# Moving the block means of v from the sync queue to GpSimd's DMA queue in a fused attention, expert and feed-forward kernel

## The chip, the cores and the metric

One core of a Trainium2 chip runs the whole program. The metric is device time in microseconds (us) of one execution; three executions of the kernel before are given, and one execution was also taken by the hardware profiler. The engines are TensorE (PE in the profile), VectorE (DVE), ScalarE (ACT), GpSimd (POOL) and SyncE (SP). SP and POOL also issue DMAs: those of SP are the queue "q1 hardware_dynamic" of the profile, those of POOL "q0 software_dynamic".

## The reference, cut to what matters

Attention over 2 batches of 8 heads, 768 positions of 64 numbers. Each position looks at the 31 positions of a band around it and at 24 summaries, one for each block of 32 positions. A block's summary key is the maximum of its keys, its summary value the mean of its values:

```python
k_sum = k.reshape(B, H, nb, block, D).max(axis=3)
v_sum = v.reshape(B, H, nb, block, D).mean(axis=3)
...
scores_all = np.concatenate([scores_l_m, scores_s], axis=-1)
...
v_all = np.concatenate([v, v_sum], axis=2)
return np.matmul(a, v_all)
```

The 1536 resulting tokens of 512 numbers go through a mixture of 8 experts (one per token, 512 to 1024 to 512) and then through a second feed-forward layer (512 to 2048 to 512). The change touches the attention alone, and in it the way of `v_sum` into the matrix product.

## The kernel before

**Attention.** Two heads lie side by side on the 128 partitions: that makes 8 pairs of heads, n = 0 to 7. A pair's 768 queries are 12 tiles of 64, worked on in groups of 4 tiles: three groups a pair, g = 0, 1, 2. Group i = 3n + g; the last group of the last pair is cut in two, so there are 25. The order of all work is written out by hand in the loop `for i in range(G)` (line 569). Iteration i transposes the exponentials of group i-2 (`do_t`), makes the scores of group i (`do_s`, line 360), the output product of group i-3 (`do_o`, line 401), the transposes of the output of group i-4 (`do_x`, line 429) and the gate product of group i-5. Each engine takes its instructions strictly in the order in which this loop names them, and waits at one until its inputs are there.

**What the output product reads.** `vw` holds, for one pair, on 24 partitions the block means, repeated for each of the 12 tiles, and on 96 partitions the windows of v, which a load (`load_v`, line 294) brings. There are three `vw` buffers, used in turn. The means come about in four steps. `vsum(n)` adds up the 32 values of a block: on DVE for n = 0 and 1, from n = 2 on in five halving steps on POOL (line 307), from `vk`, a second layout of v that `load_vk` (line 291) brings, with the block and the quarter of the columns on 96 partitions. `vmean(n)` scales by 1/32 on DVE (line 312) and issues on SP a DMA that brings the 96 x 32 means to 24 partitions of 128 numbers (`vt<-vs`, line 314): 96 runs of 128 bytes, in all 12 KB. `put_vsum(n)` issues on SP a DMA that writes each of the 24 rows twelve times into `vw` (`vw<-vt`, line 317): 288 runs of 512 bytes, 144 KB. The second DMA needs what the first one wrote, so SP waits for it to land before it issues the second.

**What else SP issues.** At the start of a pair (g = 0), right behind `put_vsum(n)`: keys and queries of pair n+2 (`wf<-in_kt` 128 x 800, `wf<-in_qt` 128 x 768, lines 260 and 261), `vk` of pair n+2 (96 x 1024) and the windows of pair n+1 (96 x 1548). At g = 2 it stores the finished output of pair n-1 to memory in two DMAs of 192 KB (line 420). Each SP DMA also waits until the one issued eight earlier has landed. `put_vsum(n)` stands at iteration 3n and is needed by `do_o` of iteration 3n+3; `vmean(n+1)` stands at g = 2 of pair n, `vsum(n+1)` at g = 1. POOL also copies the keys of each group into place (`kt<-wf`, line 282), two iterations ahead of their use. At iteration 18 SP begins to load the first expert's weights (`load_ahead`, lines 129 and 134), whose rounding copies run on DVE (line 563) from iteration 21 on, and the first gather of tokens (line 161) is an indirect DMA on POOL's queue.

**After the attention** come the routing of the tokens, 13 slots of 128 tokens through the experts, and the second layer; the functions of the change are not called there.

Of the kernel before, what the change touches and what calls it, by code (L numbers as in the profile page):

```python
# [26 lines left out]
P = 128  # L27
# [14 lines left out]
# columns of the float32 constants  # L42
# [44 lines left out]
def tile_kernel(ctx: ExitStack, tc: tile.TileContext, a, out, dbg=None):  # L87
# [3 lines left out]
    # ---- pools that live through the kernel  # L91
# [19 lines left out]
    # ---- moe2 weights: float64 bits to float32  # L111
# [46 lines left out]
    # ---- a slot of 128 tokens of one expert  # L158
# [61 lines left out]
    # ================= attention =================  # L220
# [5 lines left out]
    with ExitStack() as ax:  # L226
# [69 lines left out]
        # means of v over the blocks: [block, quarter of the columns] on the partitions, then [block]  # L296
# [13 lines left out]
        def vmean(n):  # L310
            vs = vss[n]
            nc.vector.tensor_scalar(vs, vs, 1.0 / BLK, None, op0=ALU.mult)
            vt = vts[n] = vb.tile([NB, P], F32, name="vt")
            nc.sync.dma_start(vt.rearrange("n (c d) -> n c d", c=4), vs)

        def put_vsum(n, t0=0):
            nc.sync.dma_start(vws[n % 3][0:NB, t0:, 0:P], vts[n].unsqueeze(1).broadcast_to([NB, NT - t0, P]))
# [3 lines left out]
        # the tensor engine gets to its full clock  # L321
# [32 lines left out]
        def do_s(i):  # L354
            n, t0, c = groups[i]
            kt, qb = kts[n % 2], qbs[n % 2]
            pb = ps_s.tile([P, 512], F32, name="ps", tag="ps")
            ps = pb[:, 0:c * NK].rearrange("p (c k) -> p c k", k=NK)
            for u in range(c):
                nc.tensor.matmul(ps[:, u], qb[:, t0 + u], kt[:, t0 + u], start=True, stop=True)  # L360
            spare[i] = pb[:, 4 * NK:]
            sm = wk.tile([P, c, NK], F32, name="sm", tag="sm")
            mx = wk.tile([P, c], F32, name="mx", tag="mx")
            # the negated scaled scores, and the least of them
            for u in range(c):
                nc.vector.tensor_tensor_reduce(sm[:, u], ps[:, u], msk[:, (t0 + u > 0) + (t0 + u == NT - 1)], -0.125, 3e38,
                                               op0=ALU.add, op1=ALU.min, accum_out=mx[:, u:u + 1])
            sp[i] = sm, mx
# [95 lines left out]
        # of every token: experts as [taken | later than the taken], expert-major  # L464
# [22 lines left out]
        # The first token's expert comes first. Its weights are loaded ahead, and its first 128 tokens  # L487
        # of the first batch are gathered before the second batch is through: beside column sums of
        # the scores (iterations 18 to 21).
        def first_slot(i, x):  # L490
# [7 lines left out]
            elif i == 20:  # L498
# [5 lines left out]
                def after():  # L504
                    r6 = vb.tile([P, 6], F16, name="r6", bufs=1)
                    nc.vector.tensor_scalar(r6, cum[:, 0, 0], x[:, 0:1], None, op0=ALU.add)
                    # what the first slot lacks, and where the second one begins
                    nc.vector.tensor_scalar(few, x[0:1, 1:2], P - 0.5, None, op0=ALU.is_lt)
                    nc.vector.tensor_scalar(row1, x[0:1, 1:2], float(P), None, op0=ALU.min)
                    nc.vector.tensor_scalar(lack[:, E:E + 1], x[0:1, 1:2], -float(P), 0.0, op0=ALU.add, op1=ALU.min)  # L510
                    nc.vector.tensor_scalar(lack[:, 0:1], lack[:, E:E + 1], -1.0, None, op0=ALU.mult)
                    nc.vector.tensor_tensor(t6, tok[:, 0:6], oh[:, 0, 0, 0], op=ALU.mult)
                    nc.vector.tensor_tensor(a6, io12[:, :, 0:6], r6.unsqueeze(1).broadcast_to([P, P, 6]), op=ALU.is_equal)
# [55 lines left out]
        for i in range(G):  # L569
# [58 lines left out]
            if g == 0:  # L628
                if 0 < n < 8:
                    put_vsum(n)  # L630
# [5 lines left out]
            if 0 < n < 7 and g == 2:  # L636
                vmean(n + 1)
            if 0 < n < 7 and g == 1:
                vsum(n + 1)
            while xst:  # L640
# [57 lines left out]
    # ================= routing =================  # L698
# [21 lines left out]
    with ExitStack() as rx:  # L720
# [24 lines left out]
        # position of every token in the order by expert  # L745
# [32 lines left out]
        # the second slot begins with the 129th token in the order, if the first slot is a full one  # L778
# [11 lines left out]
    def tables():  # L790
        s5 = [1, NREG, E]
        # slots of 128 tokens of one expert: expert of each
# [12 lines left out]
        # as it is numbered outside  # L805
# [7 lines left out]
        # first row of each slot; what lies past the last one goes to rows of its own  # L813
# [13 lines left out]
        # gate of every token  # L827
# [16 lines left out]
    def w_split(j):  # L844
        wh = whs[j] = st.tile([P, 1024], F32R, name="st4", tag="st4") if j < 2 else w2p.tile([P, 1024], F32R, name=f"wh{j}", tag=f"wh{j}")
        nc.scalar.copy(wh, wf[j])
        # it takes the place of a chunk that is already split
# [4 lines left out]
    # ================= mixture of experts =================  # L852
    with mx_:
# [77 lines left out]
        # dense rows that the first 11 and 12 slots have filled for good, however the tokens are spread:  # L931
        # at most 8 of them are not full
# [67 lines left out]
    # ================= second feed-forward =================  # L1000
    with ExitStack() as fx:
# [9 lines left out]
        # relu(g a)^2 = g^2 relu(a)^2 as every gate is positive  # L1011
# [24 lines left out]
        def z_mm(i):  # L1036
# [13 lines left out]
            if i == NI - LAST:  # L1050
                # the other window's tiles are read no more
# [57 lines left out]
def lay_out(q, k, v, moe_modality_id, moe_w_gate, moe_modality_bias, moe_w1, moe_w2, moe2_w_in, moe2_w_out):  # L1109
    """The arrays as the program takes them: the inputs' own values, moved and padded."""  # L1110
# [52 lines left out]
```

## Time and profile before

| What | us |
|---|---|
| Median of the 3 runs | 573.24 |
| The 3 runs | 569.95, 574.92, 573.24 |
| Span of the profiled execution, first to last instruction | 569.4 |
| PE busy in that span | 533.9 |
| PE idle at line 401 for `vw<-vt`, in total | 10.8 |

The profile gives the span of one execution and not what lies around it; the lowest of the runs is 0.55 above that span and the median 3.84. Times in rows are us from the start of the span unless they are marked ns.

### The profile page before, as it was taken

How to read it: one execution, taken by the hardware profiler on the slowest of the kernel's cores; microseconds unless marked ns; L12 is line 12 of the kernel's file. 1: busy time of each engine (PE TensorE's matmuls, PEld its weight loads, DVE VectorE, ACT ScalarE, POOL GpSimd, SP SyncE). 2: the span in 40 equal slices, each digit the busy share in tenths (PEclk: the TensorE clock that was granted, in tenths of full speed). 3: DMA queues.
4: the chain of work that ended last, by engine and by line, in shares of the span. 5: the costliest groups of instructions: out<-in, count | busy, mean ns of one | idle time of the engine just before them, and what ended most of it. 6: DMA issues, size and time to landing. Idle time of an engine off the chain costs nothing. (4 is left out here: it accounts for less than half of the span.)

```text
span 569.4 us, 8409 instructions
## 1 busy us (share of the span) xinstructions
PE 533.9 (94%) x2676; PEld 442.1 (78%) x2676; DVE 293.1 (51%) x836; ACT 223.6 (39%) x454; POOL 100.7 (18%) x115
## 2 busy tenths in 40 slices
PE   7795987979999999999889999999999999999995
PEld 6795976858878688888678888888888888888884
DVE  5885898571646953444968886423223223222230
ACT  5975886522225422223653445223222223221220
POOL 3333444640111500000317000002000000200002
PEclk8988899888999999999999999999999999999998
DMA  7795978603668644448519010001000000100001
GB/s 218 194 258 130 240 195 259 202 20 112 133 183 309 211 147 142 137 134 272 209 45 335 17 37 18 20 0 39 37 1 0 1 1 20 55 1 0 1 18 55
DMA packets 39829, 62.72 MB, mean 110 GB/s; under 512 B 19586, under 2 KB 22446, under 8 KB 39770
## 3 DMA queue, kind: packets, MB, share of 16 engines
q1 hardware_dynamic: 37386, 55.48, 32.6%
q0 software_dynamic: 2384, 6.56, 3.5%
q8 instruction: 23, 0.38, 0.3%
q14 instruction: 36, 0.29, 0.2%
HBM read 51.09 MB, written 9.71 MB: 107 GB/s over the span
## 5 line engine op out<-in xcount | busy, mean ns | idle before, releaser
L1049 DVE TENSOR_TENSOR g<-r 128x512 f32<-128x512 f32 x48 | 33.2, 691 | 106.0 <-ACT r L1047 106.0
L1047 ACT ACTIVATE r<-pz 128x512 f32<-128x512 f32 x48 | 28.7, 597 | 111.4 <-PE pz L1045 111.4
L1071 PE MATMUL pu<-wf,gh 128*128 128x512 f32 x180 | 70.5, 392 | 0.0
L1072 PE MATMUL pu<-wh,gl 128*128 128x512 f32 x156 | 61.6, 395 | 0.0
L1070 PE MATMUL pu<-wh,gh 128*128 128x512 f32 x156 | 61.5, 394 | 0.0
L1080 POOL DMA_INDIRECT out<-o,order_i x12 | 11.7, 976 | 236.8 <-DVE o L1079 215.4
L1044 PE MATMUL pz<-yt0h,wf 128*128 128x512 f32 x128 | 50.5, 395 | 0.0
L1058 ACT CAST gh<-g 128x512 fp32r<-128x512 f32 x45 | 28.0, 621 | 54.4 <-DVE g L1049 50.0
L1059 DVE TENSOR_TENSOR gl<-g,gh 128x512 fp32r<-128x512 f32 x45 | 31.2, 693 | 30.9 <-ACT gh L1058 28.9
L1043 PE MATMUL pz<-yt0h,wh 128*128 128x512 f32 x112 | 44.5, 397 | 0.0
L401 PE MATMUL po<-vw,pts 120*128 120x129 f32 x192 | 29.7, 297 | 15.4 <-DMA vw<-vt 10.8
L1045 PE MATMUL pz<-yt0l,wh 128*128 128x512 f32 x112 | 43.7, 390 | 0.0
L204 DVE TENSOR_TENSOR hl<-pt,hh 128x512 fp32r<-128x512 f32 x24 | 16.6, 690 | 47.7 <-ACTq L712 30.6
L177 PE MATMUL py<-w2l,hh 128*128 128x512 f32 x96 | 38.2, 398 | 2.9 <-DVE w2l L165 2.6
L178 PE MATMUL py<-w2h,hl 128*128 128x512 f32 x96 | 38.5, 401 | 1.6 <-DVE hl L204 1.4
L1071 PEld LDWEIGHTS pu<-wf,gh 128*128 128x128 f32 x180 | 33.8, 188 | 8.0
L401 PEld LDWEIGHTS po<-vw,pts 120*128 120x128 f32 x192 | 26.0, 206 | 17.8 <-issue 8.5
L176 PE MATMUL py<-w2h,hh 128*128 128x512 f32 x96 | 39.2, 409 | 0.0
L176 PE MATMUL ph<-w1h,xh 128*128 128x512 f32 x96 | 38.9, 405 | 0.0
L177 PE MATMUL ph<-w1l,xh 128*128 128x512 f32 x96 | 38.1, 397 | 0.0
L178 PE MATMUL ph<-w1h,xl 128*128 128x512 f32 x96 | 37.9, 395 | 0.0
L1072 PEld LDWEIGHTS pu<-wh,gl 128*128 128x128 f32 x156 | 29.3, 188 | 7.0
(239 smaller groups left out, 1129.5 us busy)
## 6 DMA issues: line engine op xcount, KB each, us to landing
st<-in_w SPq DMA_DIRECT2D x24, 512.0 KB
rw<-in_w SPq DMA_DIRECT2D x16, 512.0 KB
wf<-in_w SPq DMA_DIRECT2D x8, 512.0 KB
wh<-in_w SPq DMA_DIRECT2D x8, 512.0 KB
vw<-in_vw SPq DMA_DIRECT2D x7, 580.5 KB
y_dram<-ys SPq DMA_DIRECT2D x13, 256.0 KB
vk<-in_vk SPq DMA_DIRECT2D x8, 384.0 KB
wf<-in_kt SPq DMA_DIRECT2D x7, 400.0 KB
```

The source lines that it names most:

```text
L176: nc.tensor.matmul(ps, ah, bh, start=first, stop=False)
L177: nc.tensor.matmul(ps, ah, bl, start=False, stop=False)
L178: nc.tensor.matmul(ps, al, bh, start=False, stop=last)
L401: nc.tensor.matmul(po[-1][:, v, 0:129], pts[:, u + v], vw[:, t0 + u + v], start=True, stop=True)
L1043: nc.tensor.matmul(pz, wh[:, c], yh[:, k], start=k == 0, stop=False)
L1044: nc.tensor.matmul(pz, wl[:, c], yh[:, k], start=False, stop=False)
L1045: nc.tensor.matmul(pz, wh[:, c], yl[:, k], start=False, stop=k == 3)
L1049: nc.vector.tensor_tensor(g, r, r, op=ALU.mult)
L1059: nc.vector.tensor_tensor(gl, g, gh.bitcast(F32), op=ALU.subtract)
L1070: nc.tensor.matmul(acc[t], gh[:, c], wh, start=j == 0, stop=False)
L1071: nc.tensor.matmul(acc[t], gh[:, c], wl, start=False, stop=False)
L1072: nc.tensor.matmul(acc[t], gl[:, c], wh, start=False, stop=j == NCH - 1)
```

## The change

`vmean` and `put_vsum` of pair 0 stay as they were. For pairs 1 to 7 both DMAs are issued on POOL's queue, and for pairs 2 to 7 the scaling by 1/32 runs on POOL too. `vmean(n+1)` now stands right behind `vsum(n+1)`, at g = 1 of pair n, and `put_vsum(n+1)` at g = 2 of pair n, one iteration sooner than before. For pair 1 `vmean` stays at iteration 3 (its scaling on DVE, its DMA on POOL), and `put_vsum(1)` stands at iteration 4, behind the `vsum(2)` and `vmean(2)` of that iteration. The rest of the diff only blanks comment lines; behind the change the lines stand two further down.

```diff
         def vmean(n):
             vs = vss[n]
-            nc.vector.tensor_scalar(vs, vs, 1.0 / BLK, None, op0=ALU.mult)
+            (nc.vector if n < 2 else nc.gpsimd).tensor_scalar(vs, vs, 1.0 / BLK, None, op0=ALU.mult)
             vt = vts[n] = vb.tile([NB, P], F32, name="vt")
-            nc.sync.dma_start(vt.rearrange("n (c d) -> n c d", c=4), vs)
+            (nc.gpsimd if n else nc.sync).dma_start(vt.rearrange("n (c d) -> n c d", c=4), vs)
 
         def put_vsum(n, t0=0):
-            nc.sync.dma_start(vws[n % 3][0:NB, t0:, 0:P], vts[n].unsqueeze(1).broadcast_to([NB, NT - t0, P]))
+            (nc.gpsimd if n else nc.sync).dma_start(vws[n % 3][0:NB, t0:, 0:P], vts[n].unsqueeze(1).broadcast_to([NB, NT - t0, P]))
...
             if g == 0:
-                if 0 < n < 8:
-                    put_vsum(n)
                 if 0 < n < 6:
                     load_kq(n + 2)
                     load_vk(n + 2)
                 if 0 < n < 7:
                     load_v(n + 1)
-            if 0 < n < 7 and g == 2:
-                vmean(n + 1)
+
             if 0 < n < 7 and g == 1:
                 vsum(n + 1)
+                vmean(n + 1)
+            if i == 4:
+                put_vsum(1)
+            if 0 < n < 7 and g == 2:
+                put_vsum(n + 1)
```

On POOL, around iterations 4 and 5, before (a name's first number is its buffer, `kt0` and `kt1` being those of even and odd pairs; the number behind the underscore only tells tiles apart):

```order
L282 COPY kt0_117<-wf_213 128x4x96
L307 ISA
L307 TENSOR_TENSOR vt16_383<-vk_248 96x512
L307 TENSOR_TENSOR vt8_385<-vt16_383 96x256
L307 TENSOR_TENSOR vt4_387<-vt8_385 96x128
L307 TENSOR_TENSOR vt2_389<-vt4_387 96x64
L307 TENSOR_TENSOR vs_382<-vt2_389 96x32
L282 COPY kt0_117<-wf_213 128x4x96 x2
L282 COPY kt1_118<-wf_329 128x4x96
```

The same place on POOL now; `vt_326` and `vs_278` are the means of pair 1, `vt_392` and `vs_381` those of pair 2, `vw1_122` the buffer of pair 1:

```order
L314 DMA vt_326<-vs_278 24x4x32
L282 COPY kt0_117<-wf_213 128x4x96
L307 ISA
L307 TENSOR_TENSOR vt16_382<-vk_248 96x512
L307 TENSOR_TENSOR vt8_384<-vt16_382 96x256
L307 TENSOR_TENSOR vt4_386<-vt8_384 96x128
L307 TENSOR_TENSOR vt2_388<-vt4_386 96x64
L307 TENSOR_TENSOR vs_381<-vt2_388 96x32
L312 TENSOR_SCALAR vs_381<-vs_381 96x32
L314 DMA vt_392<-vs_381 24x4x32
L317 DMA vw1_122<-vt_326 24x12x128
L282 COPY kt0_117<-wf_213 128x4x96
```

The DMA that puts the means of pair 1 in place now stands on POOL behind the whole sum of pair 2, its scaling and its first DMA; the key copies follow behind it.

On SP, from the load of `vk` of pair 2 to the loads of pair 4, before:

```order
L291 DMA vk_248<-in_vk 96x1024
L314 DMA vt_326<-vs_278 24x4x32
L317 DMA vw1_122<-vt_326 24x12x128
L260 DMA wf_329<-in_kt 128x800
L261 DMA wf_330<-in_qt 128x768
L291 DMA vk_333<-in_vk 96x1024
L294 DMA vw2_123<-in_vw 96x1548
L314 DMA vt_443<-vs_382 24x4x32
L420 DMA x_dram_65<-xo_299 64x12x64 x2
L317 DMA vw2_123<-vt_443 24x12x128
L260 DMA wf_499<-in_kt 128x800
L261 DMA wf_500<-in_qt 128x768
```

The same stretch on SP now:

```order
L291 DMA vk_248<-in_vk 96x1024
L260 DMA wf_328<-in_kt 128x800
L261 DMA wf_329<-in_qt 128x768
L291 DMA vk_332<-in_vk 96x1024
L294 DMA vw2_123<-in_vw 96x1548
L420 DMA x_dram_65<-xo_299 64x12x64 x2
L260 DMA wf_499<-in_kt 128x800
L261 DMA wf_500<-in_qt 128x768
L291 DMA vk_503<-in_vk 96x1024
L294 DMA vw0_121<-in_vw 96x1548
```

Two DMAs of each pair have left SP, and with them the wait between them: the loads of a pair now stand directly behind the store of two pairs earlier.

## Rows read from the trace of the kernel before

**Rows 1.** The page's head: the span of the profiled execution.
```profile
span 569.4 us, 8409 instructions
```
**Rows 2.** Busy time by stretch, granted clock (PEclk), DMA share, GB/s.
```profile
50.00:60.00 10.00, 5.87 (x28) 5.90 (x29) 2.60 (x8) 3.50 (x11) 1.84 (x3) 0.66 0.76 206
60.00:70.00 10.00, 10.00 (x92) 9.92 (x91) 8.56 (x48) 8.34 (x26) 4.05 (x8) 1.00 0.89 240
300.00:400.00 100.00, 100.00 (x443) 81.44 (x442) 58.49 (x105) 36.62 (x56) 12.94 (x13) 1.00 0.19 66
```
**Rows 3.** Waits of 0 to 126 us: us in total, times, longest.
```profile
PE po L401 <- DMA vw<-vt: 10.8, 5, 5.5
...
DVE w1h L563 <- DMA wf<-in_w: 1.0, 1, 1.0
```
**Rows 4.** Waits of SP's DMA queue: us in total, times, longest.
```profile
SPq L317 <- DMA vt<-vs: 33.9, 7, 8.5
```
**Rows 5.** Timeline of PE: start, us, instruction, idle before it.
```profile
28.07 1.13 PE L401 MATMUL po<-vw,pts 120*128 120x129 f32 x8 [1.78 <-DMA vw<-vt]
...
46.53 0.38 PE L429 MATMUL px<-cst,xo 128*128 128x128 f32 x2
...
54.13 2.06 PE L401 MATMUL po<-vw,pts 120*128 120x129 f32 x8 [5.50 <-DMA vw<-vt]
55.99 0.63 PE L429 MATMUL px<-cst,xo 128*128 128x128 f32 x2
...
60.76 0.38 PE L429 MATMUL px<-cst,xo 128*128 128x128 f32 x2
...
73.02 0.38 PE L429 MATMUL px<-cst,xo 128*128 128x128 f32 x2
...
95.98 0.38 PE L429 MATMUL px<-cst,xo 128*128 128x128 f32 x2
...
100.28 1.41 PE L401 MATMUL po<-vw,pts 120*128 120x129 f32 x8 [2.65 <-DMA vw<-vt]
101.48 0.64 PE L429 MATMUL px<-cst,xo 128*128 128x128 f32 x2
```
**Rows 6.** Timeline of SP's DMA issues.
```profile
18.96 0.32 SPq L291 DMA_DIRECT2D vk<-in_vk  x1
20.62 0.81 SPq L314 DMA_DIRECT2D vt<-vs  x1
24.70 0.81 SPq L317 DMA_DIRECT2D vw<-vt  x1
...
39.85 0.83 SPq L314 DMA_DIRECT2D vt<-vs  x1
...
50.64 0.84 SPq L317 DMA_DIRECT2D vw<-vt  x1
```
**Rows 7.** The scaling on DVE, all 8: busy, mean ns, idle before.
```profile
L312 DVE TENSOR_SCALAR vs<-vs 96x32 f32<-96x32 f32 x8 | 2.4, 296 | 1.5 <-POOL vs L307 1.4
```
**Rows 8.** Timeline of POOL: a sum, a key copy, and two gathers.
```profile
23.86 1.28 POOL L307 TENSOR_TENSOR vt<-vk 96x512 f32<-96x512 f32 x1 [5.99 <-DMA vk<-in_vk]
...
26.91 0.24 POOL L307 TENSOR_TENSOR vs<-vt 96x32 f32<-96x32 f32 x1
...
29.48 0.51 POOL L282 COPY kt<-wf 128x384 f32<-128x384 f32 x1 [1.44 <-PE px L429]
...
91.28 1.15 POOL L161 DMA_INDIRECT xg<-x_dram,ix  x1 [6.78 <-DVE ix L520]
...
122.42 0.99 POOL L161 DMA_INDIRECT xg<-x_dram,order_i  x1 [3.42 <-DVE nf L777]
```
**Rows 9.** DMA queues of 91.3 to 95.7: packets, MB, share of 16 engines.
```profile
q1 hardware_dynamic: 1192, 1.46, 101.5%
q0 software_dynamic: 3, 0.01, 0.7%
```
**Rows 10.** DMA queues of 124 to 125, with no other traffic.
```profile
q0 software_dynamic: 48, 0.20, 78.5%
```

## The prediction

> **What bounds the kernel now.** I read the span first [rows 1], then the busy times by stretch, then who waited for whom, then the timelines of the three engines that the change touches, and last the DMA queues. From the stretches the reader sees two regimes [rows 2]. In 300 to 400 us PE is busy for all of the 100 us at the full granted clock: there only TensorE's own work counts, and a microsecond won or lost earlier is carried to the end unchanged. In 50 to 60 us, inside the attention, PE is busy for 5.87 of 10 us and its granted clock is 0.66, a mean of time at 1.2 and at 2.4 GHz, where 60 to 70 has 10.00 and 1.00. So the change can win or lose only in the attention, by PE's waits and the slow clock behind them.
>
> The waits say for what: PE stood 10.8 us at the output product (L401) for `vw<-vt`, five times, at the longest 5.5 us [rows 3]. The timeline shows the large three: 1.78 us before 28.07, 5.50 us before 54.13 and 2.65 us before 100.28 [rows 5]; the other two share the remaining 0.9. Behind that wait stands SP's own: it held its queue 33.9 us, in seven waits, until `vt<-vs` had landed, before it could issue `vw<-vt` [rows 4]. The worst case is issued at 39.85 and lands so late that its successor leaves at 50.64 [rows 6]. That successor lands 54.13 - 50.64 = 3.49 us after its issue begins, the first one 28.07 - 24.70 = 3.37 [rows 5, 6].
>
> **The beat.** The transposes at L429 come once an iteration. From iteration 13 (60.76) to 17 (73.02) they are 12.26 / 4 = 3.07 us apart [rows 5], which I take as the beat without a stall: a pair of heads, three iterations, takes 9.2 us. I measure stalls against it, since that also counts the slow clock that follows one.
>
> **What goes.** The transposing DMA is issued one iteration sooner and `vw<-vt` too, so from pair 2 on the means have some four iterations, 12 us, from the second DMA to the use, where they had three; and nobody on SP waits for them. I take all stalls from pair 2 on as gone:
> - Iteration 12: 55.99 - 46.53 = 9.46, less 3.07: 6.4 us.
> - Iteration 13, at the slow clock: 60.76 - 55.99 = 4.77, less 3.07: 1.7 us.
> - Iteration 24: 101.48 - 95.98 = 5.50, less 3.07: 2.4 us [all rows 5].
> - DVE waits 1.0 us for the first expert's weights [rows 3]. That load stands on SP behind `put_vsum(6)`; when SP no longer waits it is issued some us sooner. 1.0 us goes, since DVE's rounding copy stands ahead of the next scores.
> - Six of the eight scalings leave DVE, at a mean of 0.296 us [rows 7]: 1.8 us of DVE work. DVE is the late engine in a few iterations only; between 0 and 1.8 I take 0.4, and 0 would do the range no harm.
>
> Sum of the gains: 6.4 + 1.7 + 2.4 + 1.0 + 0.4 = 11.9 us. What is late next at the beat is no single engine: PE is at 10.00 of 10 us, DVE and ACT at 8.56 and 8.34 [rows 2].
>
> **What comes: pair 1's means are later.** POOL now works in this order: it issues `vt` of pair 1, sums pair 2, scales, issues `vt` of pair 2, and only then issues `vw<-vt` of pair 1. The sum starts when its `vk` is there, at 23.86, and its last step ends at 26.91 + 0.24 = 27.15 [rows 8]. Nothing ahead of it makes that `vk` earlier: its load leaves SP at 18.96 [rows 6], in front of everything that has changed on SP. The scaling on POOL is not in the trace; from the step of the same 96 x 32 shape I take 0.24 us, from DVE's 0.16 at the least to 0.9 at the most. A plain DMA issued on POOL is not there either; the nearest rows are the gathers, 0.99 and 1.15 us of POOL [rows 8], and SP's 0.81 [rows 6]. I take 1.3 us with the gap behind it, and 0.8 and 2 as ends. So the DMA that SP issued at 24.70 leaves POOL at 27.15 + 0.24 + 1.3 = 28.7, 4.0 us later.
>
> When it lands is the largest unknown, since no DMA of this kind has been seen on POOL's queue. Lower bound: 3.4 us after issue, as on an empty SP queue: 32.1. Upper bound: it queues behind all that SP has issued by then. SP, freed of its wait at 20.62 to 24.70, has issued the loads of pair 3 (with the windows of pair 2: 1.75 MB), the stores of pair 0 (0.38 MB) and three loads of pair 4 (1.17 MB), by the shapes in the order: 3.30 MB. The row of 60 to 70 moves 240 GB/s at a share of 0.89 [rows 2], so 270 when full: 12.2 us from about 23 on, and some 2.5 us to move 288 runs and report: 38. The gathers show where between the ends: with no other traffic the one issued at 122.42 moves in 124 to 125 [rows 8, 10], whereas the one issued at 91.28 has by 95.7 moved 3 packets while SP's queue moved 1192 [rows 8, 9]. A queue of its own is thus no way past SP's traffic; it cost that gather some 3 us. I take 28.7 + 3.4 + 2.9 = 35.0. The output product of iteration 6, which began at 28.07, then begins at 35.0, 6.9 us later (4.0 to 10 at the ends). The slow clock behind that stall is there before too.
>
> The Trainium skill (DMA: Bandwidth & Descriptors, section Queues, rings and completion order) has each DMA engine go round between the queues that have work, a packet at a time. By that, POOL's small DMA would be served beside SP's loads and land near the lower bound; the row of 91.3 to 95.7 does not look like that, and I keep it as a rival.
>
> **The sum.** 569.4 - 11.9 + 6.9 = 564.4 for the profiled execution. The page has no launch overhead, and the lowest run lies 0.55 above its span, the median 3.84; taken from the median of 573.24, the 5.0 us leave 568.2 us.
>
> **What is queued behind the new waits.** On POOL the second DMA waits for the first to land, with a key copy and the next pair's sum behind it. Per pair POOL has three key copies of 0.51, 3.3 of summing, 0.24 of scaling, and from the first issue to the second the landing, L, with a copy inside it, then 1.3 of issue: about 5.8 + L against the beat's 9.2. Below L = 3.4 it keeps pace; above, it falls back by the rest, from a lead of about 10 us (pair 2's first DMA leaves at 27.4, and with L = 5 the second at 32.4, to land at 36; the means are wanted at 35 + 9.2 + 1.7 for a slow clock as in iteration 13, 46). In rows L is 24.70 - 20.62 = 4.1 at the best and 50.64 - 39.85 = 10.8 at the worst.
>
> **The rivals.**
> - *POOL's queue is served at once.* Pair 1's means land at 32.1; the loss is 4.0, the net 7.9: 565.3. For it: the lower bound is what an empty queue gives, and POOL's requests are small. Against it: the gather of 91.28.
> - *The same DMA engines, so the same queue.* The landing is 38, the loss 9.9, the net 2.0: 571.2. For it: rows 9, and that SP's loads now come in closer sequence. Against it: the gather did move before SP's store was through. The Trainium skill (DMA: Bandwidth & Descriptors, section Issuing engines are not separate DMA queues) speaks for this one: issuing from another engine saves only the issuing time, since the same engines move the data.
> - *GpSimd becomes the bound (slower).* If L is 8 on average, POOL needs 13.8 us a pair; it falls back 4.6 us on each of five pairs, 23 in all, and with the lead of 10 used up PE waits 13 us in the last pairs: 568.2 + 13 = 581.2. It decides from L = 3.4 + 10 / 5 = 5.4 on, and costs over 1% from 3.4 + 20.8 / 5 = 7.6 on. For it: SP's seven waits of 33.9 us [rows 4] are 4.8 each, on top of the issues themselves, so about 6; one was 10.8, behind the small writes to `o_dram` that stay. Against it: when PE waits, SP's loads thin out and L falls.
> - *The loads bring nothing forward.* If the time won in the attention is given back where PE next waits for weights or routing, the change is worth nothing, about 573. Against it: PE's full 100 us in 300 to 400.
>
> **How the numbers follow.** My forecast (own range 565.5 to 571) 0.40; POOL at once 0.22; same queue 0.20; GpSimd the bound 0.13; given back 0.05. A measurement tells about 1% from no change here, that is 567.5 and 579.0. Faster by more: nearly all of the second case, 0.20, and somewhat under half of the first, 0.17: 0.37. Slower by more: most of the fourth, 0.10. The rest, 0.53, is within 1%. The range leaves out the far part of the fourth case and the best tail of the second: 563.5 to 577.
>
> **What would show it.** Right: PE's waits on `vw<-vt` shrink to one before iteration 6, with the product starting near 35; SP has no wait for `vt<-vs` after pair 0; iterations 12, 13 and 24 come at about 3.1 us. Wrong: that start is before 31 or after 39; waits on `vw<-vt` at pairs 4 to 7; or POOL's waits for `vt<-vs` over 6 us on the mean.

## The result

The changed kernel takes 575.53 us in the median against 572.07 us for the kernel before: a ratio of 1.0057, with a 95% interval of 1.0036 to 1.0078. It is 0.6% slower where I forecast 0.9% faster. The profiled execution has a span of 573.7 us, 4.3 us longer than [rows 1]. All rows and stretches below are of one execution of each kernel, while the 20 runs of the changed kernel spread from 571.68 to 578.35; whether every run has its stalls in the same iterations is not shown.

The head of the page and its first part, for the changed kernel:

```profile
span 573.7 us, 8426 instructions
...
PE 533.5 (93%) x2676; PEld 442.5 (77%) x2676; DVE 292.5 (51%) x830; ACT 223.4 (39%) x454; POOL 112.9 (20%) x135
```

POOL is busy for a fifth of the span, so its work is not what bounds the kernel; where it stands in its order is another matter. The waits of 0 to 130 us, to be held against [rows 3]:

```profile
POOL vw L317 <- DMA vt<-vs: 12.7, 3, 6.2
...
PE po L401 <- DMA vw<-vt: 10.7, 1, 10.7
...
PE ps L360 <- POOL kt L282: 2.1, 1, 2.1
```

PE's five waits for `vw<-vt` have become one by that name, as forecast, but that one is 10.7 us, as long as the five together; a second one stands further down under another name. There is a new wait of PE for a key copy of POOL, and DVE's wait for `wf<-in_w` is gone. The timeline of PE, to be held against [rows 5]:

```profile
37.34 2.06 PE L401 MATMUL po<-vw,pts 120*128 120x129 f32 x8 [10.68 <-DMA vw<-vt]
...
57.50 0.39 PE L429 MATMUL px<-cst,xo 128*128 128x128 f32 x2
...
63.18 0.38 PE L429 MATMUL px<-cst,xo 128*128 128x128 f32 x2
...
72.16 0.39 PE L429 MATMUL px<-cst,xo 128*128 128x128 f32 x2
...
75.44 1.21 PE L360 MATMUL ps<-kt,qb 128*128 128x120 f32 x8 [2.06 <-POOL kt L282]
...
83.28 2.06 PE L401 MATMUL po<-vw,pts 120*128 120x129 f32 x8 [0.76 <-DMA x_dram<-xo]
...
90.45 0.38 PE L429 MATMUL px<-cst,xo 128*128 128x128 f32 x2
...
103.03 0.38 PE L429 MATMUL px<-cst,xo 128*128 128x128 f32 x2
...
106.66 0.38 PE L429 MATMUL px<-cst,xo 128*128 128x128 f32 x2
...
115.00 0.27 PE L429 MATMUL px<-cst,xo 128*128 128x128 f32 x1
```

Read as intervals against the kernel before: the product of iteration 6 begins at 37.34, where it was 28.07: 9.3 us lost. Iterations 12 and 13 together (57.50 to 63.18) take 5.68 us, where 46.53 to 60.76 was 14.23: 8.55 won. Iteration 24 (103.03 to 106.66) takes 3.63, where it was 5.50: 1.87 won. But iterations 17 to 19 (72.16 to 90.45) now take 18.3 us. In them PE waits twice: 2.06 us before 75.44 for a key copy, and 0.76 before 83.28 at the product that needs pair 5's means. The profile puts the second wait down to a store, but the broadcast of these means was issued at 74.20 and took 8.8 us to land, to 83.0, so I read it as a wait for `vw<-vt`. Three more transposes of the kernel before give the rest of the account:

```profile
69.73 0.39 PE L429 MATMUL px<-cst,xo 128*128 128x128 f32 x2
...
80.28 0.39 PE L429 MATMUL px<-cst,xo 128*128 128x128 f32 x2
...
109.88 0.27 PE L429 MATMUL px<-cst,xo 128*128 128x128 f32 x1
```

There the same three iterations took 10.55 us (69.73 to 80.28): 7.7 lost. The last transpose of the attention is 5.1 us later, and the span 4.3.

What these short waits do to the clock is in the stretches (columns as in [rows 2]):

```profile
30.00:40.00 10.00, 2.67 (x13) 2.70 (x13) 0.66 (x4) 0.09 (x1) 5.87 (x12) 0.50 1.03 243
...
70.00:80.00 10.00, 7.93 (x57) 7.70 (x57) 7.09 (x36) 7.62 (x24) 5.10 (x10) 0.82 1.05 269
80.00:90.00 10.00, 9.24 (x44) 8.94 (x43) 6.55 (x34) 4.91 (x15) 6.20 (x12) 0.50 0.95 225
300.00:400.00 100.00, 100.00 (x443) 81.45 (x442) 60.06 (x106) 37.34 (x57) 13.60 (x13) 1.00 0.20 69
```

Behind the wait of 2.06 us, from 80 to 90 us PE is busy for 9.24 of 10 us, with the wait of 0.76 in it, at a granted clock of 0.50, the lower level of 1.2 GHz: two waits of 2.8 us together cost 7.7. In 30 to 40 the DMA engines are full while PE stands. In 300 to 400 us PE is busy throughout, so nothing is given back there; of the 5.1 us at the last transpose 0.8 are gone by the end of the span. POOL's timeline, and then SP's:

```profile
28.98 0.70 POOL L314 DMA_DIRECT2D vt<-vs  x1 [0.31 <-POOL vs L312]
29.68 0.68 POOL L317 DMA_DIRECT2D vw<-vt  x1
...
34.30 0.66 POOL L317 DMA_DIRECT2D vw<-vt  x1 [3.43 <-DMA vt<-vs]
...
62.85 1.29 POOL L307 TENSOR_TENSOR vt<-vk 96x512 f32<-96x512 f32 x1 [4.21 <-DMA vk<-in_vk]
...
66.83 0.66 POOL L314 DMA_DIRECT2D vt<-vs  x1 [0.29 <-POOL vs L312]
...
74.20 0.67 POOL L317 DMA_DIRECT2D vw<-vt  x1 [6.18 <-DMA vt<-vs]
74.87 0.96 POOL L282 COPY kt<-wf 128x384 f32<-128x384 f32 x2
```
```profile
23.00 0.38 SPq L291 DMA_DIRECT2D vk<-in_vk  x1
23.47 0.38 SPq L294 DMA_DIRECT2D vw<-in_vw  x1
25.92 1.37 SPq L420 DMA_DIRECT2D x_dram<-xo  x2
27.34 2.14 SPq L260 DMA_DIRECT2D wf<-in_kt  x1
...
50.49 1.29 SPq L420 DMA_DIRECT2D x_dram<-xo  x2
...
53.73 0.63 SPq L291 DMA_DIRECT2D vk<-in_vk  x1
```

SP indeed waits no longer for `vt<-vs` after pair 0. It runs ahead instead and has the last loads of pair 3 (23.00, 23.47), the store (25.92) and the first load of pair 4 (27.34) out before POOL issues pair 1's broadcast (29.68). That broadcast then takes 37.34 - 29.68 = 7.7 us to be used, where SP's took 3.4. In the second stall the key copies (74.87), which the scores at 75.44 waited for, stand behind a broadcast (74.20) that waited 6.18 us for its transposing DMA.

### The profile page after: what moved, and what is told of

Read it like the earlier page. It is cut to its first block, busy times and chain, and to the rows that moved or that the text cites. A ratio compares the mean times of both kernels' runs of the same rounds, so it can differ in the third digit from the quotient of the medians.

```text
span 573.7 us, 8426 instructions
## 1 busy us (share of the span) xinstructions
PE 533.5 (93%) x2676; PEld 442.5 (77%) x2676; DVE 292.5 (51%) x830; ACT 223.4 (39%) x454; POOL 112.9 (20%) x135
## 5 line engine op out<-in xcount | busy, mean ns | idle before, releaser
L1049 ACT ACTIVATE r<-pz 128x512 f32<-128x512 f32 x48 | 28.7, 597 | 110.2 <-PE pz L1047 110.2
L401 PE MATMUL po<-vw,pts 120*128 120x129 f32 x192 | 30.7, 304 | 16.1 <-DMA vw<-vt 10.7
L401 PEld LDWEIGHTS po<-vw,pts 120*128 120x128 f32 x192 | 26.8, 212 | 18.3 <-issue 10.8
L360 PE MATMUL ps<-kt,qb 128*128 128x120 f32 x192 | 29.8, 305 | 6.1 <-issue 3.2
```

Of the source, the lines that this page charges most:

```text
L401: nc.tensor.matmul(po[-1][:, v, 0:129], pts[:, u + v], vw[:, t0 + u + v], start=True, stop=True)
```

## The experiments

Edits are given against the changed kernel unless the text says otherwise. Ratios are to the kernel before, with 95% intervals; "iteration n" is the interval that ends with its transpose.

**Pair 1 alone back on SP.**

```
-            (nc.gpsimd if n else nc.sync).dma_start(vt.rearrange(...
+            (nc.gpsimd if n > 1 else nc.sync).dma_start(vt.rearrange(...
-            (nc.gpsimd if n else nc.sync).dma_start(vws[n % 3][0:NB, ...
+            (nc.gpsimd if n > 1 else nc.sync).dma_start(vws[n % 3][0:NB, ...
...
             if g == 0:
+                if n == 1:
+                    put_vsum(1)
...
-            if i == 4:
-                put_vsum(1)
```


> Edit: of the changed kernel, pair 1 alone goes back to the sync queue (both its DMAs, where they stood before); pairs 2 to 7 stay on GpSimd. Three theories. (A) The loss has one root, pair 1's late broadcast, which put the product of iteration 6 about 10 us later; the second stall, at iterations 17 to 19 (7.75 us), is its child: the late product makes the store of x(1) late (50.49 on SP where it was 40.72), and the loads of pair 5 stand behind that store. Then both go: the transpose of iteration 6 comes at 29 to 30 instead of 39.19, iterations 17 to 19 at about 3.1 us each, and the span is the one before less the gains of iterations 12, 13 and 24: 569.4 - 10.9 = 558.5, 556 to 562. (B) The second stall stands by itself, from GpSimd's order (key copies behind a wait for vt): iteration 6 as in A, but iterations 17 to 19 lose 5 to 8 us again: 564 to 567. (C) Pair 1 has nothing to do with the loss (it is the traffic or the scaling): no change from 573.7, 572 to 576.

Measured: 573.79 us, 1.0043 (1.0016 to 1.007), span 573.1. Iteration 6's stall is gone (its transpose comes at 29.98), yet almost nothing is won. Three rows of PE:

```profile
29.01 1.13 PE L401 MATMUL po<-vw,pts 120*128 120x129 f32 x8 [0.79 <-DMA vw<-vt]
...
37.83 1.34 PE L360 MATMUL ps<-kt,qb 128*128 128x120 f32 x8 [3.80 <-POOL kt L282]
...
80.56 2.06 PE L401 MATMUL po<-vw,pts 120*128 120x129 f32 x8 [2.63 <-DMA x_dram<-xo]
```

So (A) falls: the second stall is no child of the first. Other stalls came too: iteration 8 takes 7.9 us, iterations 12 and 13 again 7.2 and 4.7, iterations 18 and 19 6.8 and 5.7. (B) named the place; the time of 564 to 567 that it gave is missed, since it knew nothing of iterations 8, 12 and 13. Its mechanism shows at iteration 8: the key copy that the scores at 37.83 waited for stands behind a broadcast that had waited 6.12 us. At iterations 18 and 19 it is the broadcast itself that is late. The span lies in (C)'s range of 572 to 576, but its reason does not hold, since iteration 6's stall went. The last row names a store as releaser, but the broadcast of that pair, issued at 72.31, was still moving its packets until about 79, so I read its landing there as 80.56 - 72.31 = 8.2 us.

**Pair 1's broadcast ahead of pair 2's sum, on POOL.**

```
             if i == 3:
                 vmean(1)
+                put_vsum(1)
...
-            if i == 4:
-                put_vsum(1)
```


> Edit: of the changed kernel, GpSimd issues pair 1's broadcast right behind pair 1's transposing DMA, ahead of the sum of pair 2; queue and everything else as changed. It parts the two terms of pair 1's delay: GpSimd's order (issue at 29.68 instead of about 25) and the landing beside the sync queue's loads (7.7 us instead of 3.4). If the order is all (landing 3.4 us from an issue at about 25), iteration 6's transpose comes at 30 and the span is near 559 with the second stall gone, near 566 with it there. If the landing is most, the issue is still at 25 to 27 but it lands 7 us later, at 32 to 34: iteration 6's transpose at 34 to 36, span 564 to 570. If the transposing DMA itself lands later on GpSimd's queue (over 6 us), the issue is at 27.5 to 29 and little is won: 570 to 574.

Measured: 576.15 us, 1.0095 (1.0055 to 1.0134), span 574.3; the broadcast leaves at 27.24 and the product begins at 34.76, 7.5 us behind. Against the kernel before, 2.5 us of its lateness are the later issue and 4.1 the longer landing, nearest to the second case; in the changed kernel it is 5.0 and 4.3, so POOL's order and the landing count about alike there. The 2.6 us that the first stall gives back are lost again behind it (iterations 14 and 15 take 8.0 and 6.1), so its time is missed too.

**Broadcasts of pairs 2 to 7 one iteration later.**

```
-            if 0 < n < 7 and g == 2:
-                put_vsum(n + 1)
+            if 1 < n < 8 and g == 0:
+                put_vsum(n)
```


> Edit: of the changed kernel, GpSimd's broadcast of pairs 2 to 7 is issued one iteration later, behind the next key copy, so that no key copy of the pair stands behind its wait for the transposing DMA. Pair 1 as changed. (B) If GpSimd's order makes the second stall, the wait of the scores on the key copies (2.06 us) and the slow clock behind it go: iterations 17 to 19 at about 3.1 us, span 573.7 - 7.75 = 566. (A) If the means of pair 5 are late by themselves, since their vk landed only at 62.85, the stall only changes its place: the product of iteration 18 waits for the broadcast of pair 5 instead, which still leaves at about 74 to 75; 570 to 575. Iteration 6 is at 39 in both.

Measured: 578.20 us, 1.0134 (1.0079 to 1.0189), span 574.6. Iteration 17 takes 3.25 us, so the key copies were what it waited for; but iteration 18 then waits for the broadcast (7.6 us), and the last pair's, now late, costs iteration 24 7.8. The key copies behind the wait are where the lateness shows first, not where it comes from; the product at 83.28 of the changed kernel shows the same.

**Scaling back on VectorE.**

```
-            (nc.vector if n < 2 else nc.gpsimd).tensor_scalar(vs, ...
+            nc.vector.tensor_scalar(vs, ...
```


> Edit: of the changed kernel, the scaling of all pairs is on VectorE again; both DMAs and their order as changed. Theories A and B give the scaling no part in the loss: it is 0.30 us on GpSimd and 0.17 on VectorE, so 573 to 575 (VectorE's queue may hand the means over some tenths later). (C) If the scaling on GpSimd was what delayed pair 1's broadcast, the product of iteration 6 comes 1 us or more earlier and the span is 571 or less.

Measured: 574.95 us, 1.0057 (1.0021 to 1.0093): the time is that of the changed kernel, as A and B had it. But half of (C)'s sign came: the product of iteration 6 begins 4.0 us sooner, and the stalls stand elsewhere (iterations 14 and 15 take 7.2 and 8.3, iteration 19 again 7.2). Pair 1's broadcast and that product:

```profile
29.45 0.66 POOL L317 DMA_DIRECT2D vw<-vt  x1
```
```profile
33.37 2.06 PE L401 MATMUL po<-vw,pts 120*128 120x129 f32 x8 [6.68 <-DMA vw<-vt]
```

The broadcast leaves only 0.23 us sooner, so it is not the scaling's own time that was won: the landing took 3.9 us instead of 7.7. SP had issued its last load 6.2 us before it (23.23), and the store and the loads of pair 4 only behind it (30.43 on). Whether the edit brought that about or this one execution did is open.

**The writes to `o_dram` later, in the kernel BEFORE, and two companions.**

```
-            nc.sync.dma_start(o_dram[N:], zr)
...
         while xst:
             store_x(*xst.pop(0))
+        nc.sync.dma_start(o_dram[N:], zr)
```


> Edit: of the kernel BEFORE, only the 128 writes of 4 bytes to o_dram (L254) are issued later, behind the last store of x. (D) The stall that the change was to remove, iterations 12 and 13 (8.1 us over the beat), was made by those writes: the transposing DMA of pair 3 is issued 2.4 us behind them on the same queue (37.49, 39.85) and its successor leaves at 50.64, with no packet on any queue from 48 to 50.6. Then that DMA lands in about 4 to 5 us, iterations 12 and 13 come at 3 to 4 us, and the span is 569.4 - 8.1 = 561.3 (560 to 564). (E) The stall is of the two chained DMAs on the sync queue as such, and the writes have no part: 568 to 571.

> Edit: of the CHANGED kernel, the same writes to o_dram issued behind the last store of x. In its trace they were issued at 40.64, with nothing behind them on the sync queue until 50.49, and the transposing DMA of pair 3 was on another queue and already issued. (D) They cost nothing there: 572 to 575. If they are what made iteration 18 late too, 566 or less.

> Edit: pair 1 on the sync queue as in the run with pair 1 alone undone (573.1), and the writes to o_dram issued behind the last store of x. In that run iterations 12 and 13 lost 5.7 us over the beat, behind a transposing DMA of pair 4 that took 9.9 us to land, in a stretch where the DMA engines were 91% busy for 111 GB/s right behind those writes. (D) That stall goes: 573.1 - 5.7 = 567.4 (565 to 569), with the losses of iterations 8, 9, 18 and 19 left. (F) If the landing was long only because loads stood beside it, 571 to 575.

Measured: in the kernel before 568.77 us, 0.9942 (0.9899 to 0.9986); in the changed kernel 575.71, 1.0093 (1.0053 to 1.0132), no gain; with pair 1 on SP 572.14, 1.0014 (0.998 to 1.0048). (In every kernel with the writes late the lines behind them stand one up.) The stall of iterations 12 and 13 in the kernel before was thus in part no matter of the means' place at all. First the DMA packets of the kernel before from 46 to 50.6 us, in which SP stood waiting for the transposing DMA of pair 3; then SP's rows of the run with the writes moved:

```profile
DMA packets 21, 0.01 MB, mean 3 GB/s; under 512 B 20, under 2 KB 20, under 8 KB 20
```
```profile
40.87 0.83 SPq L313 DMA_DIRECT2D vt<-vs  x1
...
48.30 0.84 SPq L316 DMA_DIRECT2D vw<-vt  x1
```

The wait from the one DMA to the next falls from 10.8 to 7.4 us, and iterations 12 and 13 from 14.2 to 9.5. (D) has the right cause with too large a size, and its span of 560 to 564 is missed (567.7): of the 8.1 us over the beat 4.7 belong to the writes, the rest to a landing of 7 us that is left. With pair 1 on SP (f3) both iterations come at 2.84 us; its span fell by 4.6, a little less than the 5.7. What had held iteration 12 in its parent run was pair 3's broadcast on GpSimd's queue, issued at 45.13, 2.2 us behind the writes (42.94), and used at 56.86; the broadcast of pair 4, which I had put down to a late transposing DMA, waited for PE at its end.

**The changed order, both DMAs on SP.**

```
-            (nc.gpsimd if n else nc.sync).dma_start(vt.rearrange(...
+            nc.sync.dma_start(vt.rearrange(...
...
-            (nc.gpsimd if n else nc.sync).dma_start(vws[n % 3][0:NB, ...
+            nc.sync.dma_start(vws[n % 3][0:NB, ...
```


> Edit: the changed kernel's order (transpose one iteration sooner, broadcast one sooner) with both DMAs on the sync queue; scaling stays on GpSimd. It parts the move in time from the queue. (G) The cause is the move in time: the transposing DMA is now issued one iteration behind the pair's 1.75 MB of loads instead of two, and lands with them: iteration 6 and a later stall stay, 571 to 577. (H) The cause is GpSimd's queue, that is landings of 4 to 9 us beside the sync queue's loads and key copies behind its waits: on one queue the broadcast stands ahead of the next loads again, so 560 to 567, with iteration 6 at 30 or sooner.

Measured: 577.04 us, 1.0109 (1.0054 to 1.0165), span 575.2, iteration 6 at 36.2. (G): the earlier place loses on either queue. On SP the transposing DMAs take some 7 us behind the loads (67.33 to the broadcast at 74.95, for one), and the broadcast of pair 1 now stands behind pair 3's loads and behind the whole sum of pair 2 there too. It is late by its issue, though, not by its landing. Its row (that of pair 2 is in it) and the product:

```profile
30.35 3.92 SPq L317 DMA_DIRECT2D vw<-vt  x2
```
```profile
34.31 2.06 PE L401 MATMUL po<-vw,pts 120*128 120x129 f32 x8 [6.77 <-DMA vw<-vt]
```

It leaves 5.65 us later than in the kernel before and takes 4.0 us, with the last load 3.8 us ahead of it (26.52) and the store behind it (34.32). A run with both DMAs on GpSimd at their old places was not made.

**Less traffic beside it.**

```
+            if n > 1:
+                kqs[n] = kqs[n - 2]
+                return
             kp, qp = kqs[n] = ...
-            if n > 1:
-                nc.sync.dma_start(kp, a["kt"][n])
-                nc.sync.dma_start(qp, a["qt"][n])
```


> Edit: the CHANGED kernel without the key and query loads of pairs 2 to 7 (they reuse the tiles of pairs 0 and 1, so the attention of those pairs is left out): 0.78 of 1.75 MB of each pair's loads go, all else stays. (J) The means are late because GpSimd's two DMAs land beside the sync queue's loads (medians 4.9 and 6.5 us): with the traffic nearly halved they land in about 3 to 4 us each, iteration 6's transpose comes at 31 to 34 instead of 39.2 and iterations 17 to 19 at 3 to 4 us each, last transpose of the attention at 103 to 107 instead of 115. (K) GpSimd's queue is slow by itself, whatever stands beside it: landings of 5 us and more, iteration 6 at 37 or later, last transpose at 111 or later.

> Edit: the same loads left out of the kernel BEFORE, as the control. (J) There, too, the transposing DMA stands behind the loads (4.1 to 10.8 us, mostly 6 to 7): it lands in 3 to 5 us, SP's seven waits of 33.9 us fall below 20, and the last transpose comes at 100 to 106 instead of 109.9, with what is left of iterations 12 and 13 due to the writes to o_dram. (K) Landings and waits as before, last transpose at 108 to 111.

Measured, one execution each: 569.99 us with the change, 560.22 without it. In the kernel before SP's waits for `vt<-vs` fall from the 33.9 us of [rows 4] to 12.4, and the last transpose comes at 97.5. In the changed kernel iterations 17 and 18 come at 2.84 and 3.06 us, but iteration 19 takes 7.00, the last transpose comes at 107.75 (between the two ranges), and iteration 6 is still at 35.9: its broadcast, issued at 27.24, is used at 34.06, 6.8 us later. These two leave it open between (J) and (K).

**No loads beside it; another queue.** The first of these two also has the edit just shown.

```
                 if 0 < n < 6:
                     load_kq(n + 2)
-                    load_vk(n + 2)
-                if 0 < n < 7:
-                    load_v(n + 1)
+                    vks[n + 2] = vks[n]
+                if n == 1:
+                    load_v(2)
```


> Edit: the CHANGED kernel without any of the loads of pairs 3 to 7 and without the key and query loads of pair 2 (tiles of earlier pairs are reused, so the attention of these pairs is left out). Beside pair 1's broadcast only the store of x(0) and the small DMAs move. (J) If other traffic makes the landing, it is 3 to 4.5 us. (K) If GpSimd's queue is slow for this broadcast by itself, it is 6 us or more again.

```
             if i == 4:
-                put_vsum(1)
+                nc.scalar.dma_start(vws[1][0:NB, :, 0:P], vts[1]...)
```


> Edit: the changed kernel with pair 1's broadcast alone issued from ScalarE's queue, at the same iteration (its transposing DMA and all other pairs stay on GpSimd). All loads are there. Its nearest run is the one with the broadcast ahead of pair 2's sum on GpSimd (issued 27.24, product 7.5 us behind). (J) If the loads beside it make the landing, whichever queue it stands on, it is 6 to 8 us again, iteration 6's transpose at 34 to 37. (K) If GpSimd's queue is the slow part, it lands in 3.4 to 4.5 us: iteration 6 at 30 to 32.

Without loads (601.27 us, of which nothing is read but the landing), the broadcast on POOL and its product:

```profile
27.73 0.67 POOL L317 DMA_DIRECT2D vw<-vt  x1
```
```profile
31.86 2.06 PE L401 MATMUL po<-vw,pts 120*128 120x129 f32 x8 [4.84 <-DMA vw<-vt]
```

On ScalarE's queue (580.18 us) with all loads, the same two:

```profile
26.53 1.41 ACTq L639 DMA_DIRECT2D vw<-vt  x1
```
```profile
34.26 2.06 PE L401 MATMUL po<-vw,pts 120*128 120x129 f32 x8 [6.75 <-DMA vw<-vt]
```

4.1 us on POOL with little but the store beside it, 7.7 us on ScalarE's queue with the loads: (J). It is the traffic, and whose queue the broadcast stands on does not show. Sixteen kernels of this document have all loads and a product of iteration 6 that waits for it. In ten of them SP's last load had left 3.8 to 6.5 us before the broadcast, and the product began 3.3 to 4.0 us after its issue: nine times on SP's queue, once on GpSimd's. In the other six the last load had left 0.1 to 2.2 us before, and it took 7.3 to 8.2: five times on GpSimd's queue, once on ScalarE's. Each is one execution. What mattered for pair 1 in the kernel before was that the broadcast stood AHEAD of the loads, which SP could not issue before it.

**The transposing DMA ahead of the loads (kernel BEFORE, writes late).** In the first, pair n+2's sum goes to g = 2 of pair n and its transposing DMA to g = 0 of pair n+1, between the broadcast and the loads; in the second, which the diff shows, the sum goes there as well:

```
             if g == 0:
                 if 0 < n < 8:
                     put_vsum(n)
+                if 1 < n < 7:
+                    vsum(n + 1)
+                    vmean(n + 1)
...
-            if 0 < n < 7 and g == 2:
-                vmean(n + 1)
-            if 0 < n < 7 and g == 1:
-                vsum(n + 1)
+            if i == 5:
+                vmean(2)
+            if i == 4:
+                vsum(2)
```


> Edit: of the kernel BEFORE, with the writes to o_dram behind the last store of x (568.8 alone, 0.994): from pair 3 on the sum of a pair is made one iteration sooner (last iteration of the pair two ahead) and the transposing DMA leaves on the sync queue in the first iteration of the pair ahead, behind the broadcast of that pair and AHEAD of the next loads, not behind them. (J) If landings beside the loads are the cause, the transposing DMA lands in about 4 us, SP holds no loads back for it and the broadcast finds it landed: iterations 12, 13, 18 and 24 lose 6 us less than in the run with the writes moved alone, 560 to 564. If GpSimd's sum one iteration sooner blocks the key copies behind its wait for vk, 568 to 575.

> Edit: as the run before, but the sum stands in the first iteration of the pair ahead too, so that SP waits some 4 us for it with the next loads behind. (J) Landing as there (about 4 us), but the loads leave some 3 to 4 us later: 560 to 567. If the loads' issue is what bounds the iterations, 568 to 574.

Measured: 577.92 us, 1.0105 (1.0071 to 1.0138), and 577.48, 1.0068 (1.0034 to 1.0103). Both lose, and by more than either range said. POOL's wait in the first:

```profile
POOL vt L306 <- DMA vk<-in_vk: 45.6, 6, 9.0
```

POOL stands for `vk`, the third of the loads, up to 9 us at a time, and SP for POOL's sum: the loads of one pair wait, through the sum, for the loads of the pair before.

**`vk` first of the loads.**

```
                 if 0 < n < 6:
+                    load_vk(n + 2)
                     load_kq(n + 2)
-                    load_vk(n + 2)
```


> Edit: the kernel before with the writes to o_dram late, pair n+1's sum in the first iteration of pair n, its transposing DMA ahead of the next loads (as in the run that took 577), and each pair's vk load first of its loads instead of third. If the loop load of vk, landing 7 to 9 us, sum 3.5 us, next loads (12.8 us a pair against the beat's 9.2) was what cost, it shrinks by the landing to about 9: iterations 8, 10, 12, 18 at 3 to 4 us, 558 to 565. If vk lands as late in first place, or the key loads behind it become late, 570 to 577.

> Edit: the kernel before with the writes to o_dram late (568.8) and the vk loads first; nothing else. In that run SP's loop (broadcast, loads, transposing DMA that lands 6 to 7 us behind the loads) takes 10.4 to 11.2 us a pair, and the sum is done before it is wanted: vk first does not shorten it, 567 to 570. If the sum was what was late, 562 to 566.

Measured: with the second version above 562.86 us, 0.9839 (0.9768 to 0.991); with the writes late alone 566.74, 0.9885 (0.9844 to 0.9925). Both beat both kernels; the intervals overlap, so which of the two is better stays open, and so does whether `vk` first wins anything beside the writes alone (0.9942, 0.9899 to 0.9986). Behind the second version of the edit above, `vk` first makes the difference between 1.0068 and 0.9839. SP's rows of one pair of the first, and a stretch:

```profile
52.31 1.02 SPq L316 DMA_DIRECT2D vw<-vt  x1
55.18 0.83 SPq L313 DMA_DIRECT2D vt<-vs  x1
56.06 0.50 SPq L290 DMA_DIRECT2D vk<-in_vk  x1
...
61.76 0.85 SPq L316 DMA_DIRECT2D vw<-vt  x1
...
64.43 0.85 SPq L313 DMA_DIRECT2D vt<-vs  x1
```
```profile
50.00:60.00 10.00, 10.00 (x91) 9.90 (x90) 9.06 (x51) 9.66 (x31) 4.32 (x8) 1.00 0.90 265
```

A pair now takes 64.43 - 55.18 = 9.25 us on SP, the beat itself, and PE is at its full clock for the stretch in which the kernel before had 5.87 of 10 us [rows 2].

**`vk` first in the changed kernel; the writes back in their place in the version that beat both.**

> Edit: the CHANGED kernel with each pair's vk load first of its loads instead of third, for pairs 3 to 7; nothing else. If the second stall comes from the late start of pair 5's sum (its vk landed at 62.85, 9.1 us behind its issue), that sum starts 3 to 5 us sooner, iterations 17 to 19 lose 5 us or more less, and the span is 566 to 569. If the two landings beside the loads are enough for it, the stall stays or comes in another pair: 571 to 576. Iteration 6 is at 38 to 40 in both, since pair 1's means are not touched.

> Edit: the version that beat both (562.9: sum in the first iteration of the pair ahead, transposing DMA ahead of the loads, vk first, writes to o_dram late) with the writes to o_dram back in their old place. If they hold up what stands behind them on the sync queue whatever the order, iterations 9 to 13 lose 4 to 5 us: span 563 to 565. If they only did so for a transposing DMA right behind them, no change: 557 to 561.

Measured: 576.05 us, 1.007 (1.003 to 1.0111), span 571.5; and 570.31 us, 0.9979 (0.9951 to 1.0008). In the changed kernel the sum of pair 5 starts at 58.90 instead of 62.85, and iterations 17 to 19 take 10.8 us instead of 18.3: the late `vk` made that stall. But iterations 21 and 22 then take 5.6 us each, and the median does not move: the stall went to the next pair. Of the reordered version's gain about 7.4 us (570.31 - 562.86) hang on the writes being out of the way, and with them back its interval (0.9951 to 1.0008) includes no change; iterations 11 to 13 take 17.2 us with them and 9.3 without.

## Why the prediction was wrong

- *SP no longer waits, and iterations 12, 13 and 24 come back to the beat*: right. 8.1 us were forecast for 12 and 13, 8.55 came; 2.4 for 24, 1.87 came; the wait for the first expert's weights (1.0) went. The scaling's 0.4 is not to be seen. What I did not see is that more than half of the largest gain was owed to the small writes ahead of the DMA, not to its place.
- *Pair 1's DMA leaves POOL at 28.7*: 29.68. The scaling took 0.30 and the first DMA 0.70 us, less than the 1.3 taken; but the sum started at 24.99 instead of 23.86, since the load of its `vk` left SP at 20.05 instead of 18.96 (it took 4.9 us in both). I had held that this load could not move.
- *When it lands*: mis-sized. I took 3.4 + 2.9 = 6.3 us; it was 7.7, and the product began at 37.34 instead of 35.0, 9.3 us late where I had 6.9. I had 38 as the upper bound, and the rival of the same queue took it. The error was to lean toward the empty queue's 3.4: that row is of a DMA which held the loads back behind it (from 24 to 26 us the kernel before moved nothing by DMA). The change did not only move the DMA; it took away its precedence. The Trainium skill (DMA: Bandwidth & Descriptors, section Issuing engines are not separate DMA queues) has the DMAs of all issuing engines run on the same 16 DMA engines and interleave; the 7.7 us on GpSimd's queue and the 7.7 on ScalarE's agree with it. The round of packets between queues (the Trainium skill, DMA: Bandwidth & Descriptors, section Queues, rings and completion order), which I kept as a rival, did not bring the DMA near its lower bound where loads had left just before it (7.3 to 8.2 us on GpSimd's queue); where the last load had left 6.2 us before, it took 3.9.
- *What is queued behind the new waits*: this step failed, and cost 7.7 us that the sum did not have. I gave POOL a lead of about 10 us and let a landing cost only when the mean L passed 5.4. From one DMA to the next it was 5.3, 4.6, 2.4, 7.4, 4.3 and 5.5 us for pairs 2 to 7, 4.9 on the mean (for pairs 3, 4 and 7 the profile has PE end the wait, not the landing), so by my rule nothing should have happened. But POOL cannot run ahead of `vk`: for pair 5 it landed at 62.85. Its load left SP at 53.73, behind the store of x(1) at 50.49, and took 9.1 us; in the kernel before it left at 52.87 and the sum began at 58.59. A single L of 7.4, without any lead, put the key copies 2.06 us late, the broadcast behind it took 8.8 us and held the product by another 0.76, and the slow clock did the rest. The order of the queue was named in the text (a key copy behind the second DMA); its due time was not computed, nor the clock behind it.
- *From pair 2 on the means have an iteration more*: true of the place in the program, not of the time. The broadcast of pair 5 leaves POOL at 74.20; in the kernel before SP issued it no later, as its rows show:

```profile
66.34 0.84 SPq L314 DMA_DIRECT2D vt<-vs  x1
...
72.75 0.84 SPq L317 DMA_DIRECT2D vw<-vt  x1
```

- *The rival of GpSimd as the bound* had the mechanism (POOL in order, waiting for landings) with a price of 13 us and a condition on the mean that was not met; the truth lies between it and the forecast.

The account, by transposes: iteration 11 comes 10.97 us later (57.50 for 46.53), iterations 12 and 13 win 8.55, 17 to 19 lose 7.74, 20 to 23 win 3.12 (12.58 where it was 15.70), 24 wins 1.87, the rest 0.05: +5.12 at the last transpose, where I had -5.0. What stays open: what shortened iterations 20 to 23, which the forecast did not have; why POOL's broadcast still took 6.8 us with the keys and queries gone, and why the small writes held up DMAs in some runs and not in others.

## What to carry to other kernels

A wait on an in-order queue can be doing work: it holds back the transfers behind it, so a small DMA that others depend on lands on free engines. Before such a DMA is moved to another queue, ask what will be issued while it waits, and price its landing as if it stood behind all of that. What helped here was not another queue but what stood on the same one: the small writes moved out of the way, and with that the transposing DMA ahead of the loads and of the loads first the one that starts the longest chain. The order without the writes moved gave nothing clear of noise (0.9979).

## What was unexpected of the hardware

The 128 writes of 4 bytes to memory (0.5 KB in all) took 8.1 us to land in the changed kernel, in stretches of 2 us that moved 0 to 69 GB/s in all (40 to 50 us):

```profile
DMA to landing us min/median/max: 8.1/8.1/8.1
```

Behind them in the kernel before it was 10.8 us from a DMA of 12 KB to the one that waits for it, and in the last 4.6 us of these 21 packets moved on all queues together. A DMA issued on GpSimd cost it 0.66 to 0.70 us (0.83 for the first), about half of what I had taken from the gathers.
